# GQA attention into a gated MLP on one core: an earlier first half of v, later loads, statistics put behind the next weighing, and the last store issued by ScalarE

## The chip, the cores and the metric

The kernel runs on one core of one Trainium2 chip. The metric is the device time of one execution in microseconds. A core has five engines, each with its own in-order queue of instructions: TensorE (PE in the profile, with its weight loads as PEld), VectorE (DVE), ScalarE (ACT), GpSimd (POOL) and SyncE (SP), which here only issues DMAs. They wait for each other by semaphores.

## The reference

Eight batches of grouped-query attention (16 query heads on 4 key/value heads, 384 tokens, head size 64) give x of 384 x 1024 a batch. A gated MLP follows. What matters of it:

```python
attn = softmax(q @ k^T / 8)            # per head; k, v repeated for 4 query heads each
x = (attn @ v) as [B, S, 1024]
h = np.maximum(x @ w_in, 0.0)          # w_in: 1024 x 1024
u, v = h[..., :512], h[..., 512:]
mu = np.mean(v, axis=-1, keepdims=True)
var = np.mean((v - mu) ** 2, axis=-1, keepdims=True)
v_n = (v - mu) / np.sqrt(var + 1e-06)
v_s = np.einsum('ts,bsd->btd', w_spatial, v_n) + b_spatial[None, :, None]
return (u * v_s) @ w_out               # w_out: 512 x 1024
```

## The kernel before

The order of every engine's instructions is written out by hand. A main loop runs over 150 steps n. A batch b takes NU = 18 of them, from s0 = 18 b on: 6 groups m (three blocks of 128 query positions times two halves j of the heads) times 3 tiles t of keys. What a step issues, in this order:

- what `at(n, ...)` has put down for the step: DMA loads on SP's or GpSimd's queue, casts to 16 bit on GpSimd, and the DMA transposes `k_turn`, `q_turn` and `x_turn` on SP's queue;
- `scores`: two matmuls `sc` (L233, 64 rows each, side by side in the array) and one exponential of 128 x 1024 on ScalarE (L240). In batch 0 step n issues scores n + 1; later every even step issues its own and the next one's. There are two PSUM buffers `sc`;
- `weigh(b, m, hh)`, at n = s0 + 3 + 3 m + hh: twelve matmuls `av` of 65 columns (L247), then on VectorE the reciprocal `r` (L257) and the product `x` (L259). `av` has a single PSUM buffer, so the next `av` waits for `x`;
- what `turn_at(n, ...)` has put down: in the first batches transposes of k, q and x on TensorE (`kps`, `qps`, `xps`), copied out of PSUM by VectorE, and `keep_warm(4)`, four matmuls of 128 columns on the identity that nothing reads (L547);
- `run_fill(cols)`: takes matmuls of the MLP from one stream (`stream()`) until `cols` columns are paid.

The stream's order for batch 0 is v_tile(0,0), v_tile(0,1), u_tile(0,0), v_tile(0,2), u_tile(0,1), u_tile(0,2); then, per batch, the gates (`psp`), the first v_tile of the next batch, the output projection (`po`), and for later batches v_tile(b,1), v_tile(b,2) and the u blocks (`pu`). A `v_tile` is eight `pv` matmuls of 512 columns (L294), and on VectorE `vr` (L304), `stats` (L306) and the aggregate `mv` (L307). `normal(b)`, called out of the first u block (or the second u tile in batch 0), has ScalarE make `rstd` from the variance in two instructions (L314, L315), VectorE make `nmr` from it (L316), and GpSimd normalise the three tiles to `vn` (L327); in the last batch VectorE and ScalarE take one tile each.

All short-lived matmul results (`kps`, `qps`, `xps`, `wps`, `pv`, `pu`, `psp`, `po`) share one PSUM pool of three buffers, `ps_ck`. The tile `warm` is taken from it once at the start and stays held until the last `keep_warm`, at step 15.

The transposed x of batch b comes, from batch 1 on, by DMA transposes on SP's queue at steps s0 + 8, s0 + 14, s0 + 17 and s0 + 20 (one for each of the first two query blocks, two halves for the third). v_tile(b, st) reads block st. SP's queue also carries q's and k's transposes of the next batch, the loads of the batch after that (k, two halves of q, v) and the output stores.

How the fill is shared out in the first batch, with HV = 4096 columns for one v tile:

```python
run_fill(HV / 4 if 10 <= n < 14 else 2 * HV / 5 if 16 <= n else 0)   # n < NU + 3
```

Of the kernel before, what the change touches and what calls it, by code (L numbers as in the profile page):

```python
# [9 lines left out]
FP32 = mybir.dt.float32  # L10
FP16 = mybir.dt.float16
AF = mybir.ActivationFunctionType
ALU = mybir.AluOpType
# [4 lines left out]
def kernel(  # L18
# [16 lines left out]
    nc = tc.nc  # L35
    P = 128
    B, HQ, S, D = q.shape
# [4 lines left out]
    NT = S // P  # L42
# [181 lines left out]
    def scores(n):  # L224
        b, r = divmod(n, NU)
        m, t = divmod(r, NT)
        qt, j = divmod(m, 2)
        if t == 0:
            aTs[b, m] = att.tile([P, NT, 2, 512], FP16, name=f"aT_{b}_{m}", tag="aT", bufs=3)
        sc = ps_sc.tile([P, 2, 512], FP32, name=f"sc_{b}_{m}_{t}", tag="sc")  # L230
        for hh in range(2):
            half = slice(hh * D, (hh + 1) * D)
            nc.tensor.matmul(  # L233
                sc[:, hh],
                kTs[b][half, j, t * P : (t + 1) * P],
                qTs[b, j][half, qt],
                start=True,
                stop=True,
            )
        nc.scalar.activation(aTs[b, m][:, t], sc, AF.Exp, scale=scale)  # L240

    def weigh(b, m, hh):
        qt, j = divmod(m, 2)
        av = ps_av.tile([P, G, D + 1], FP32, name=f"av_{b}_{m}_{hh}", tag="av")
        for i in range(G):
            for t in range(NT):
                nc.tensor.matmul(  # L247
                    av[:, i, :],
                    aTs[b, m][:, t, hh, i * P : (i + 1) * P],
                    v1[b % 2][:, 2 * j + hh, t, 0 : D + 1],  # L250
                    start=(t == 0),
                    stop=(t == NT - 1),
                )
        if m == 0 and hh == 0:
            x16s[b] = att.tile([P, NT, NB, P], FP16, name=f"x16_{b}", tag="x16")
        r = small.tile([P, G, 1], FP32, name=f"r_{b}_{m}_{hh}", tag="r")
        nc.vector.reciprocal(r, av[:, :, D : D + 1])  # L257
        blk = 4 * j + 2 * hh
        nc.vector.tensor_tensor(  # L259
            x16s[b][:, qt, blk : blk + 2].rearrange("p k (i d) -> p (k i) d", i=2),  # L260
            av[:, :, 0:D],
            r.to_broadcast([P, G, D]),
            ALU.mult,
        )
# [23 lines left out]
    def v_tile(b, st):  # L288
        if st == 0:
            mvs[b] = small.tile([P, NT, 2], FP32, name=f"mv_{b}", tag="mv")  # L290
            v_rs[b] = []
        pv = ps_ck.tile([P, 512], FP32, name=f"pv_{b}_{st}", tag="ck")
        for kt in range(NB):
            nc.tensor.matmul(  # L294
                pv,
                x_tile(b)[:, st, kt],
                w_in16[:, kt, DH:DFF],
                start=(kt == 0),
                stop=(kt == NB - 1),
            )  # L300
            if kt < NB - 1:
                yield 512
        vr = moe.tile([P, DH], FP32, name=f"vr_{b}_{st}", tag="vr", bufs=4)
        nc.vector.tensor_scalar(vr, pv, 0.0, None, op0=ALU.max)  # L304
        stats = small.tile([P, 6], FP32, name=f"stats_{b}_{st}", tag="stats")
        nc.vector.bn_stats(stats, vr)  # L306
        nc.vector.bn_aggr(mvs[b][:, st, :], stats)  # L307
        v_rs[b].append(vr)
        yield 512

    def normal(b):
        rstd = small.tile([P, NT], FP32, name=f"rstd_{b}", tag="rstd")
        nmr = small.tile([P, NT], FP32, name=f"nmr_{b}", tag="nmr")
        nc.scalar.activation(rstd, mvs[b][:, :, 1], AF.Ln, bias=eps_t)  # L314
        nc.scalar.activation(rstd, rstd, AF.Exp, scale=-0.5)  # L315
        nc.vector.scalar_tensor_tensor(  # L316
            nmr, mvs[b][:, :, 0], -1.0, rstd, op0=ALU.mult, op1=ALU.mult
        )
        v_ns[b] = []
        for st in range(NT):  # L320
            vn = moe.tile([P, DH], FP16, name=f"vn_{b}_{st}", tag="vn", bufs=6)
            a, c = rstd[:, st : st + 1], nmr[:, st : st + 1]
            if b == B - 1 and st == 2:
                nc.scalar.activation(vn, v_rs[b][st], AF.Identity, scale=a, bias=c)
            else:
                by = nc.vector if b == B - 1 and st == 1 else nc.gpsimd
                by.tensor_scalar(vn, v_rs[b][st], a, c, op0=ALU.mult, op1=ALU.add)  # L327
            v_ns[b].append(vn)

    def uT_tile(b):  # L330
# [107 lines left out]
    def project(b, tt, half):  # L438
        last = b == B - 1
        rows = out[b].rearrange("(p t) d -> p t d", t=NT)  # L440
        if half == 0:
            osbs[b, tt] = ops.tile([P, DM], FP32, name=f"osb_{b}_{tt}", tag="osb")
        osb = osbs[b, tt]

        cuts = (512, 896, 1024) if last and tt == NT - 1 and half else (512 * half, 512 * half + 512)
        for i, (lo, hi) in enumerate(zip(cuts, cuts[1:])):
            po = ps_ck.tile([P, 512], FP32, name=f"po_{b}_{tt}_{half}_{i}", tag="ck")
            for m in range(NM):
                nc.tensor.matmul(  # L449
                    po[:, 0 : hi - lo],  # L450
                    gTs[b][:, m, tt * P : (tt + 1) * P],
                    w_out16[:, m, lo:hi],
                    start=(m == 0),
                    stop=(m == NM - 1),
                )
                if m < NM - 1:
                    yield hi - lo
            (nc.scalar.copy if half and not i else nc.vector.tensor_copy)(  # L458
                osb[:, lo:hi], po[:, 0 : hi - lo]
            )  # L460
            if last:
                nc.sync.dma_start(rows[:, tt, lo:hi], osb[:, lo:hi])
            elif half:
                nc.sync.dma_start(rows[:, tt, :], osb)
            yield hi - lo
# [66 lines left out]
    def at(n, f, *args):  # L532
        todo.setdefault(n, []).append((f, args))
# [6 lines left out]

    by_dve, by_act = nc.vector.tensor_copy, nc.scalar.copy

    warm = ps_ck.tile([P, 512], FP32, name="warm", tag="ck")

    def keep_warm(n):
        for _ in range(n):
            nc.tensor.matmul(warm[:, 0:P], ident16, ident16, start=True, stop=True)  # L547

# [27 lines left out]
    for j in range(2):  # L576
        for t in (1, 2):
            turn_at(3 * (2 * t + j) - 3, q_transposes, 0, j, t, by_dve)
    for n in (*range(10), 14, 15):
        turn_at(n, keep_warm, 4)  # L580
    at(9, cast_k, 1, pool)
    at(10, cast_q, 1, 0, pool)
# [19 lines left out]
    for b in range(B):  # L602
        s0 = NU * b
        if b >= 2:
            w0 = s0 - NU
            if b > 2:
                at(w0 - NU + 11, load_k, b)
                at(w0 - NU + 11, load_q, b, 0)
                at(w0 - NU + 11, load_q, b, 1)
                at(w0 - NU + 11, load_v, b)  # L610
            c0, c1, t0, t1 = (6, 7, 10, 12) if b > 2 else (9, 10, 12, 13)
            at(w0 + c0, cast_k, b, pool)
            at(w0 + c0, cast_q, b, 0, pool)
            at(w0 + c1, cast_q, b, 1, pool)
            at(w0 + c1, cast_v, b, pool)
            at(w0 + t0, k_turn, b)
            at(w0 + t0, q_turn, b, 0)
            at(w0 + t1, q_turn, b, 1)
        for m in range(6):
            if b == 0 or b == B - 1 and m > 3:  # L620
                turn_at(s0 + 3 * m + 5 + (m < 5 and b == 0), x_transposes, b, m)
            elif m in (1, 3):
                at(s0 + 3 * m + 5, x_turn, b, m // 2, 0, NB)
            elif m > 3:
                at(s0 + 3 * m + 5, x_turn, b, 2, 4 * (m - 4), 4 * (m - 3))
# [5 lines left out]
    def run_fill(cols):  # L631
        nonlocal owed
        owed += cols
        while owed > 0:
            owed -= next(fill, 1e9)

    for n in range(total + 6):
        for f, args in todo.pop(n, []):
            f(*args)
        if n + 1 < NU:  # L640
            scores(n + 1)
        elif n >= NU and n % 2 == 0 and n < total:
            scores(n)
            scores(n + 1)
        for hh in range(2):
            b, r = divmod(n - 3 - hh, NU)
            if n >= 3 + hh and r % 3 == 0 and b < B:
                weigh(b, r // 3, hh)
        for f, args in turns.pop(n, []):
            f(*args)  # L650
        if n < NU + 3:

            run_fill(HV / 4 if 10 <= n < 14 else 2 * HV / 5 if 16 <= n else 0)
        elif n < 2 * NU + 4:
            run_fill((4 * HV + NM * NT * S + 6 * NM * 512) / (NU + 4 - 3))
        else:
            run_fill(COLS / NU)
# [31 lines left out]
```

## Time and profile before

| | us |
|---|---|
| median of 3 runs (lowest, highest) | 251.71 (251.39, 252.03) |
| the profiled execution, its own time | 251.51 |
| its span, first to last instruction | 249.7 |

| engine | busy us | share of the span |
|---|---|---|
| TensorE matmuls | 240.9 | 96% |
| ScalarE | 169.1 | 68% |
| VectorE | 139.9 | 56% |
| GpSimd | 97.4 | 39% |

Times in all views are microseconds from the span's start; a duration that follows an operation as a mean is in nanoseconds. In the time line a row is start, length, engine, line, operation, output <- input, shapes, count, and in brackets the idle time before it with what ended it. In the chain of waits a row is start, length, engine and line. In the list of waits a row is who waited for whom: total, times, longest. In the table of windows a row is the stretch, its length, then the busy time of TensorE, its weight loads, VectorE, ScalarE and GpSimd with the numbers of instructions, the granted clock, the share of the DMA engines and GB/s. A matmul's record is longer than its turn: matmuls are pipelined, and two neighbours overlap.

### The profile page before, as it was taken

To read this page: it belongs to the slowest core of one execution; us is meant where nothing else is said; L and a number is where in the kernel's file an instruction comes from. 1 tells how busy PE (TensorE), PEld (TensorE's weight loads), DVE (VectorE), ACT (ScalarE), POOL (GpSimd) and SP (SyncE) were. 2 spreads that over 40 slices of the span, in tenths; PEclk is the share of its full clock that TensorE was granted. 3 is DMA by queue.
4 is the path that set the end of the run, shared out by engine and by line. 5 is a ranking of instruction groups with operands and counts; after the bars stand their busy time and mean duration, and the time that the engine had idled before them with its cause. 6 is when DMAs were issued, how large, how long until landed. Compare 5 with 4: busy or idle time off the path is not lost.

```text
span 249.7 us, 6038 instructions
## 1 busy us (share of the span) xinstructions
PE 240.9 (96%) x2438; PEld 126.2 (51%) x2438; DVE 139.9 (56%) x370; ACT 169.1 (68%) x217; POOL 97.4 (39%) x141
## 2 busy tenths in 40 slices
PE   7998998999999999999999999999999999999993
PEld 7564666634455445544455445544455444554551
DVE  2455777764546646375536746375536746375662
ACT  3896665777686677868686677868686687862231
POOL 2698836881034800393034800393034000350130
PEclk9999999999999999999999999999999999999999
DMA  7999998999379973996479973999474172024206
GB/s 180 269 285 252 301 281 238 289 233 265 104 145 326 173 276 66 236 274 178 168 145 333 169 273 71 206 302 175 171 151 90 24 273 45 0 46 168 84 26 230
DMA packets 73980, 46.93 MB, mean 188 GB/s; under 512 B 48112, under 2 KB 68912, under 8 KB 73952
## 3 DMA queue, kind: packets, MB, share of 16 engines
q1 hardware_dynamic: 68832, 37.63, 59.2%
q0 software_dynamic: 4080, 8.65, 13.9%
q8 instruction: 19, 0.31, 0.5%
q10 hardware_dynamic: 1040, 0.26, 0.5%
q14 instruction: 9, 0.07, 0.1%
HBM read 25.95 MB, written 12.58 MB: 154 GB/s over the span
## 4 chain that ended last, share of the span: by engine, by line
PE 91%; DVE 6%; ACT 1%; issue 1%; POOL 0%; POOLq 0%
PE av L247 17%; PE pv L294 16%; PE sc L233 15%; PE po L449 15%; PE pu L359 14%; PE psp L378 6%; PE warm L547 3%; DVE x L259 2%; DVE stats L306 1%; DVE vr L304 1%; PE pu L342 1%; PE qps L200 1%; ACT aT L240 1%; PE psp L402 1%; PE xps L275 1%
## 5 line engine op out<-in xcount | busy, mean ns | idle before, releaser
L240 ACT ACTIVATE aT<-sc 128x1024 f16<-128x1024 f32 x144 | 139.6, 1021 | 53.3 <-PE sc L233 53.1
L247 PEld LDWEIGHTS <-aT 128*128 128x128 f16 x1152 | 43.4, 97 | 32.9 <-DVE x L259 12.8
L327 POOL TENSOR_SCALAR vn<-vr,rstd,nmr 128x512 f16<-128x512 f32 x22 | 16.9, 778 | 100.0 <-DVE r L257 86.2
L247 PE MATMUL av<-v,aT 128*128 128x65 f16 x1152 | 52.4, 194 | 1.6 <-DVE x L259 1.2
L257 DVE RECIPROCAL r<-av 128x4 f32<-128x4 f32 x96 | 17.2, 179 | 58.3 <-PE av L247 57.7
L294 PE MATMUL pv<-w_in,xt 128*128 128x512 f16 x192 | 49.6, 379 | 0.0
L449 PE MATMUL po<-w_out,gT 128*128 128x512 f16 (+2 forms) x196 | 47.9, 375 | 0.0
L233 PE MATMUL sc<-qT,kT 64*128 64x512 f16 x288 | 45.4, 385 | 0.5 <-DVE qT L205 0.3
L259 DVE TENSOR_TENSOR x<-av,r 128x256 f16<-128x256 f32 x96 | 40.8, 425 | 3.4
L359 PE MATMUL pu<-xt,w_in 128*128 128x384 f16 x216 | 40.2, 326 | 0.0
L389 POOL TENSOR_TENSOR gT<-g,uT 128x384 f16<-128x384 f32 x28 | 24.7, 914 | 26.8 <-DVE g L388 26.8
L359 PEld LDWEIGHTS <-w_in 128*128 128x128 f16 x216 | 19.4, 98 | 14.2 <-issue 2.5
L170 POOL CAST q<-q 128x768 f16<-128x768 f32 (+1 forms) x36 | 24.9, 733 | 3.1 <-DMA q<-in_q_dram 3.1
L449 PEld LDWEIGHTS <-gT 128*128 128x128 f16 x196 | 16.9, 97 | 18.3 <-issue 2.9
L294 PEld LDWEIGHTS <-xt 128*128 128x128 f16 x192 | 16.1, 97 | 13.5 <-issue 0.6
L458 DVE COPY osb<-po 128x512 f32<-128x512 f32 (+1 forms) x25 | 16.7, 667 | 11.1 <-PE po L449 11.1
L233 PEld LDWEIGHTS <-kT 64*128 64x128 f16 x288 | 8.9, 94 | 26.4 <-issue 24.0
L304 DVE TENSOR_SCALAR vr<-pv 128x512 f32<-128x512 f32 x24 | 16.5, 688 | 10.2 <-PE pv L294 10.0
L458 ACT COPY osb<-po 128x512 f32<-128x512 f32 (+1 forms) x24 | 14.0, 584 | 10.6 <-PE po L449 10.5
L306 DVE BATCH_NORM_STATS2 stats<-vr 128x6 f32<-128x512 f32 x24 | 16.7, 695 | 0.8
L378 PE MATMUL psp<-wsT,vn 128*128 128x384 f16 x84 | 17.0, 327 | 0.0
L388 DVE TENSOR_TENSOR g<-psp,bias_b 128x384 f32<-128x384 f32 x28 | 14.4, 552 | 2.7 <-PE psp L378 2.7
(59 smaller groups left out, 136.2 us busy)
## 6 DMA issues: line engine op xcount, KB each, us to landing
out_dram<-osb SPq DMA_DIRECT2D x21, 512.0 KB, 2.9
q<-in_q_dram SPq DMA_DIRECT2D x10, 768.0 KB, 7.1
q<-in_q_dram POOLq DMA_DIRECT2D x4, 768.0 KB, 10.4
v<-in_v_dram SPq DMA_DIRECT2D x6, 384.0 KB, 8.7
w_in<-in_moe_w_in_dram POOLq DMA_DIRECT2D x4, 512.0 KB, 9.8
k<-in_k_dram SPq DMA_DIRECT2D x5, 384.0 KB, 4.1
out_dram<-osb SPq DMA_DIRECT2D x5, 256.0 KB, 2.0
q<-in_q_dram SPq DMA_DIRECT2D x2, 512.0 KB, 7.2
```

The costliest lines, as they stand in the source:

```text
L170: f(q16s[b, j][:, lo:hi, :, hh, :], src[:, hh, lo:hi])
L233: nc.tensor.matmul(sc[:, hh], kTs[b][half, j, t * P : (t + 1) * P], qTs[b, j][half, qt], start=True, stop=True,)
L240: nc.scalar.activation(aTs[b, m][:, t], sc, AF.Exp, scale=scale)
L247: nc.tensor.matmul(av[:, i, :], aTs[b, m][:, t, hh, i * P : (i + 1) * P], v1[b % 2][:, 2 * j + hh, t, 0 : D + 1], start=(t == 0), stop=(t ...
L259: nc.vector.tensor_tensor(x16s[b][:, qt, blk : blk + 2].rearrange("p k (i d) -> p (k i) d", i=2), av[:, :, 0:D], r.to_broadcast([P, G, D]) ...
L294: nc.tensor.matmul(pv, x_tile(b)[:, st, kt], w_in16[:, kt, DH:DFF], start=(kt == 0), stop=(kt == NB - 1),)
L306: nc.vector.bn_stats(stats, vr)
L359: nc.tensor.matmul(pu[:, 0:S].rearrange("p (t s) -> p t s", t=NT), w_in16[:, kt, m * P : (m + 1) * P], x_tile(b)[:, :, kt], start=(kt == 0 ...
L378: nc.tensor.matmul(psp[:, 0:S], v_ns[b][st][:, m * P : (m + 1) * P], wsT16[:, st, :], start=(st == 0), stop=(st == NT - 1),)
L389: nc.gpsimd.tensor_tensor(gTs[b][:, m, :], g, uTs[b][:, m, :], ALU.mult)
L449: nc.tensor.matmul(po[:, 0 : hi - lo], gTs[b][:, m, tt * P : (tt + 1) * P], w_out16[:, m, lo:hi], start=(m == 0), stop=(m == NM - 1),)
L458: (nc.scalar.copy if half and not i else nc.vector.tensor_copy)(osb[:, lo:hi], po[:, 0 : hi - lo])
```

## The change

Five things, in one diff:

- A v tile's `stats` and aggregate aren't issued at once but put into a list `due`, which is emptied after the next `weigh`, before the next v tile's `vr`, or at the head of `normal`. In the last batch they are issued at once.
- `normal` makes `minus` = -mean, which doesn't need `rstd`, in place of `nmr`; the normalisation adds `minus` and multiplies by `rstd`. The last batch makes one [128 x 1] product `ac` more, for ScalarE's tile.
- The first v tile's eight `pv` are spread over steps 6 to 11, the second's over 13 to 17, the third share over 18 to 20. Scores 13 to 17 are issued one step later, 14 with 15 and 16 with 17. `keep_warm` runs at steps 0 to 5 alone and takes a PSUM buffer anew each time.
- The loads of batches 3 to 7 are issued at step 16 of a period of 18, in place of step 11: on SP's queue behind the second half of q's transposes and the second x transpose, ahead of the last two x transposes.
- The very last store (128 columns, 64 KB) is issued by ScalarE in place of SyncE.

```diff
@@ v_tile
+        do_due()
         vr = moe.tile([P, DH], FP32, name=f"vr_{b}_{st}", tag="vr", bufs=4)
         nc.vector.tensor_scalar(vr, pv, 0.0, None, op0=ALU.max)
         stats = small.tile([P, 6], FP32, name=f"stats_{b}_{st}", tag="stats")
-        nc.vector.bn_stats(stats, vr)
-        nc.vector.bn_aggr(mvs[b][:, st, :], stats)
+
+        def statistics():
+            nc.vector.bn_stats(stats, vr)
+            nc.vector.bn_aggr(mvs[b][:, st, :], stats)
+
+        due.append(statistics)
+        if b == B - 1:
+            do_due()
         v_rs[b].append(vr)
         yield 512
 
+    due = []
+
+    def do_due():
+        while due:
+            due.pop(0)()
+
@@ normal
         rstd = small.tile([P, NT], FP32, name=f"rstd_{b}", tag="rstd")
-        nmr = small.tile([P, NT], FP32, name=f"nmr_{b}", tag="nmr")
+        do_due()
+        minus = small.tile([P, NT], FP32, name=f"minus_{b}", tag="minus")
         nc.scalar.activation(rstd, mvs[b][:, :, 1], AF.Ln, bias=eps_t)
         nc.scalar.activation(rstd, rstd, AF.Exp, scale=-0.5)
-        nc.vector.scalar_tensor_tensor(
-            nmr, mvs[b][:, :, 0], -1.0, rstd, op0=ALU.mult, op1=ALU.mult
-        )
+        nc.vector.tensor_scalar(minus, mvs[b][:, :, 0], -1.0, None, op0=ALU.mult)
+        if b == B - 1:
+            ac = small.tile([P, 1], FP32, name="ac", tag="ac")
+            nc.vector.tensor_tensor(ac, minus[:, 2:3], rstd[:, 2:3], ALU.mult)
...
-            a, c = rstd[:, st : st + 1], nmr[:, st : st + 1]
+            a, c = minus[:, st : st + 1], rstd[:, st : st + 1]
             if b == B - 1 and st == 2:
-                nc.scalar.activation(vn, v_rs[b][st], AF.Identity, scale=a, bias=c)
+                nc.scalar.activation(vn, v_rs[b][st], AF.Identity, scale=c, bias=ac)
             else:
                 by = nc.vector if b == B - 1 and st == 1 else nc.gpsimd
-                by.tensor_scalar(vn, v_rs[b][st], a, c, op0=ALU.mult, op1=ALU.add)
+                by.tensor_scalar(vn, v_rs[b][st], a, c, op0=ALU.add, op1=ALU.mult)
@@ project
             if last:
-                nc.sync.dma_start(rows[:, tt, lo:hi], osb[:, lo:hi])
+                (nc.scalar if i else nc.sync).dma_start(rows[:, tt, lo:hi], osb[:, lo:hi])
@@ the schedule
-    warm = ps_ck.tile([P, 512], FP32, name="warm", tag="ck")
-
     def keep_warm(n):
+        warm = ps_ck.tile([P, 512], FP32, name="warm", tag="ck")
         for _ in range(n):
             nc.tensor.matmul(warm[:, 0:P], ident16, ident16, start=True, stop=True)
...
-    for n in (*range(10), 14, 15):
+    for n in range(6):
         turn_at(n, keep_warm, 4)
...
-                at(w0 - NU + 11, load_k, b)
-                at(w0 - NU + 11, load_q, b, 0)
-                at(w0 - NU + 11, load_q, b, 1)
-                at(w0 - NU + 11, load_v, b)
+                at(w0 - NU + 16, load_k, b)
+                at(w0 - NU + 16, load_q, b, 0)
+                at(w0 - NU + 16, load_q, b, 1)
+                at(w0 - NU + 16, load_v, b)
@@ the main loop
-        if n + 1 < NU:
+        if n < 12:
             scores(n + 1)
-        elif n >= NU and n % 2 == 0 and n < total:
+        elif n == 13:
+            scores(n)
+        elif n % 2 == 0 and n > 13 and n < total:
             scores(n)
             scores(n + 1)
...
                 weigh(b, r // 3, hh)
+                do_due()
...
-            run_fill(HV / 4 if 10 <= n < 14 else 2 * HV / 5 if 16 <= n else 0)
+            at_n = {6: 8, 7: 8, 8: 8, 9: 8, 10: 4, 11: 4, 13: 6, 14: 6, 15: 6, 16: 4, 17: 4}
+            run_fill(HV / at_n[n] if n in at_n else HV / 3 if n >= NU else 0)
```

## The prediction

> **What bounds the kernel now.** I read the page first (busy time, clock), then the waits, then a table of windows, then the time line around every place where TensorE stands still.
>
> ```profile
> span 249.7 us, 6038 instructions
> ...
> PE 240.9 (96%) x2438; PEld 126.2 (51%) x2438; DVE 139.9 (56%) x370; ACT 169.1 (68%) x217; POOL 97.4 (39%) x141
> ...
> PEclk9999999999999999999999999999999999999999
> ...
> L240 ACT ACTIVATE aT<-sc 128x1024 f16<-128x1024 f32 x144 | 139.6, 1021 | 53.3 <-PE sc L233 53.1
> ...
> 95.28:123.34 28.06, 28.02 (x273) 13.65 (x273) 15.58 (x41) 20.83 (x28) 10.60 (x14) 1.00 0.82 205
> ...
> PE av L247 <- DVE x L259: 1.2, 3, 0.6
> ```
>
> TensorE is busy for 240.9 of 249.7 us; the next engine, ScalarE, for 169.1. The window is one batch in the steady part: 28.06 us, 28.02 of them busy on TensorE. So nothing is won by making another engine faster; only by taking work off TensorE or by ending one of its few waits. The wait named, 1.2 us in three places, is for x on VectorE. "Busy" hides more: a matmul's record outlasts its turn in the pipe, so a short stall leaves no gap. It shows when starts are compared with the pace.
>
> ```profile
> 229.86 3.45 PE pv L294 x16
> 28.74 0.54 PE sc L233 x4
> ...
> 119.12 2.10 PE L294 MATMUL pv<-w_in,xt 128*128 128x512 f16 x9
> 122.08 1.24 PE L294 MATMUL pv<-w_in,xt 128*128 128x512 f16 x5
> 123.34 0.55 PE L247 MATMUL av<-v,aT 128*128 128x65 f16 x12
> 99.66 0.60 PE L233 MATMUL sc<-qT,kT 64*128 64x512 f16 x4
> 100.28 0.54 PE L247 MATMUL av<-v,aT 128*128 128x65 f16 x12
> ...
> 99.51 0.16 DVE L316 SCALAR_TENSOR_TENSOR nmr<-mv,rstd 128x3 f32<-128x3 f32 x1 [1.45 <-ACT rstd L315]
> 99.80 0.42 DVE L259 TENSOR_TENSOR x<-av,r 128x256 f16<-128x256 f32 x1
> 121.12 0.69 DVE L304 TENSOR_SCALAR vr<-pv 128x512 f32<-128x512 f32 x1 [1.16 <-PE pv L294]
> 121.84 0.69 DVE L306 BATCH_NORM_STATS2 stats<-vr 128x6 f32<-128x512 f32 x1
> 122.67 0.15 DVE L257 RECIPROCAL r<-av 128x4 f32<-128x4 f32 x1
> 122.86 0.42 DVE L259 TENSOR_TENSOR x<-av,r 128x256 f16<-128x256 f32 x1
> ```
>
> Sixteen pv take 3.45 us, 0.216 each. Five from 122.08 are through at 123.16, but the av behind them starts at 123.34: it waits for x, which ends at 123.28, because the PSUM buffer of av is single and VectorE did vr and the statistics first. That is a stall of 0.18. Likewise four sc take 0.54, so av could start at 100.20 and starts at 100.28: x (99.80 + 0.42 = 100.22) was held up since nmr stood waiting for rstd at the head of VectorE's queue. 0.08. Together 0.26 us a batch, invisible on the page.
>
> **The change, part by part.** *Statistics behind the next weighing.* In the new program's order r and x stand ahead of stats and aggregate except in the last batch, and what takes the place of nmr needs no rstd, so VectorE doesn't stand behind ScalarE. In the first stall above, r starts when vr ends (121.81) or its av does, and x ends before 123.0, ahead of 123.16; what is late next is nothing, as stats then fills the room before the next av ends. In the second, the wait of 1.45 us is gone and x is done long before 100.20. The trace has it six times (the av of 123.34 less two and plus three periods of 28.06, from 67.2 to 207.5): 6 x 0.26 = 1.56 us off. Bounds: 1.1 (first kind alone, 6 x 0.18) to 1.6. Batch 1 has two larger ones:
>
> ```profile
> 40.23 0.55 PE L247 MATMUL av<-v,aT 128*128 128x65 f16 x12 [0.58 <-DVE x L259]
> 54.37 0.54 PE L247 MATMUL av<-v,aT 128*128 128x65 f16 x12 [0.43 <-DVE x L259]
> ```
>
> The second is a plain case of statistics ahead of x: 0.43 off. Before the first, vr, stats, aggregate and the wait for rstd stand in a row; the flush at the head of the normalisation keeps the statistics ahead of x there, and only the wait goes. I take 0.55 of it (0.4 to 0.7, with the unseen part of the stall). The third of the 1.2 us, in the last batch, stays, as the statistics aren't put off there. Batch 1: 0.98 off. The new [128x1] product in the last batch costs what nmr did (0.16) and stands in its place: 0.
>
> *The early half of v.* Eight of the first pv move from steps 10 to 13 into steps 6 to 11, the filler matmuls of steps 6 to 9, 14 and 15 go, scores 13 to 17 come a step later with 14/15 and 16/17 in pairs, and the filler's PSUM buffer is no longer held through to step 15.
>
> ```profile
> 13.39 0.48 PE av L247 x12
> 14.09 0.22 PE warm L547 x4
> 14.32 0.22 PE xps L275 x4
> 15.89 0.33 PE warm L547 x4
> 26.21 0.32 PE sc L233 x2
> ...
> 14.80 0.41 DVE L276 COPY xt<-xps 128x512 f16<-128x512 f16 x1
> ...
> 21.65 0.38 PE L275 MATMUL xps<-ident,x 128*128 128x128 f16 x4 [0.84 <-DVE qT L205]
> ```
>
> Off: four fillers of 0.22 and two of 0.33 that all lay on TensorE's path, 1.5 us; a pair costs 0.54 against twice 0.32, 0.2 for two; the wait of 0.84 for a free buffer. Some 2.6 us. On: waits for VectorE, which I follow step by step. Step 6 without its filler is through with xps at 14.31. The first pv needs the copy xt, which still ends at 14.80 + 0.41 = 15.21: it starts at 15.27, a stall of 0.95, and sc 8 stands behind it. Steps 7 to 11 are five sc (1.60), three av (1.44), a qps and an xps (four transposes each, 0.44) and seven pv (1.51): through at 20.48, with all eight pv done where before had four. Step 12 (av, qps, xps, 0.92) ends at 21.40. On VectorE vr runs from 20.65 (a record ends 0.16 after its turn) to 21.34, then r and x (122.67 to 123.28 above, 0.61) to 21.95: after sc 13 the next av waits 0.3 and ends at 22.5. Behind x come stats and aggregate (121.84 to 122.67, 0.83) and the copies of qT and xt (0.41 each), to 23.5 with their overlap, and the pv of step 13, the first of the second tile, needs that xt: another 1.0. Two pv, the pair 14/15 (with a kps), one pv: 24.9. Step 15's av needs the exponentials of score 14, ready at about 24.3 + 1.02 (a wait of 0.45); av behind it ends at 25.8; two kps, a qps and an xps (0.8) share two free buffers and so wait for VectorE's copies (0.6 to 0.8 more); two pv follow, and step 16 starts near 27.8. Pair, av, qps and four pv later, step 18 starts at 29.9, against 28.74. So the waits put on, 3.4 to 3.8, eat more than the 2.6 taken off: 1.2 later. By then 16 pv are done against 14.4 (8 and two shares of 3.2), worth 1.6 x 0.216 = 0.35, which the smaller shares of steps 18 to 20 give back. I take 0.9 us on. Bounds: 0.3 (the two long xt waits a third shorter) to 1.4 (nothing given back).
>
> The fillers were there to keep TensorE running. The first 27 took 3.06 us, 0.113 each, those later 0.22 / 4 = 0.055: it starts at half rate, though PEclk reads 9.
>
> ```profile
> 1.62 3.06 PE warm L547 x27
> ```
>
> The gap of 0.84 was followed by xps and pv at full rate. The longest new one is 0.95 with pv and av on both sides, so I put no loss of rate into the sum. The Trainium skill, "TensorE: Matmul & The Clock Gate", Part 1, says that the gate halves the clock after an idle window of some 3.4 us; by that rule too single gaps of 1 us cost nothing, though what it counts is activity over a window. The stretch from 21.7 to 27.8 has three waits, so half rate is a rival below.
>
> *Loads five steps later.* Four loads a batch (five batches) now stand on SP's queue behind qT and the second x transposition, ahead of the last two.
>
> ```profile
> 68.52 1.24 SPq L279 DMA_TRANSPOSE xt<-x  x1
> 72.74 0.88 SPq L79 DMA_DIRECT2D k<-in_k_dram  x1
> 74.92 1.98 SPq L82 DMA_DIRECT2D v<-in_v_dram  x1
> 76.99 5.65 SPq L215 DMA_TRANSPOSE qT<-q  x1
> 87.24 1.34 SPq L279 DMA_TRANSPOSE xt<-x  x1
> ...
> v<-in_v_dram SPq DMA_DIRECT2D x6, 384.0 KB, 8.7
> xt<-x SPq DMA_TRANSPOSE x26, 3.2
> ```
>
> A step is 28.06 / 18 = 1.56 us. The second x transposition, six steps behind the one at 68.52, can now go at 77.9, and the loads at 79.2 instead of 72.74: v is issued at 81.4 and lands at 90.1. The third is issued behind it and, held like qT was (5.65), is through the queue by 89; 3.2 later it has landed, 92.2 at the latest. The ninth pv of 119.12 needs it, at 120.85, here 92.79. The fourth follows a store at about 89.5 and lands at 92.7 to 93.5; it is needed three pv after 122.08, here 94.67. Hidden, with 0.6 and 1.2 us to spare: 0. The cover is thin; in batch 1, where two stores stand between, it may lack 0 to 0.7 once (I take 0.1).
>
> *Last store on ScalarE's queue.*
>
> ```profile
> 245.72 1.30 SPq L462 DMA_DIRECT2D out_dram<-osb  x3
> 245.87 0.29 DVE L458 COPY osb<-po 128x128 f32<-128x128 f32 x1 [0.18 <-PE po L449]
> ...
> out_dram<-osb SPq DMA_DIRECT2D x1, 192.0 KB, 2.2
> out_dram<-osb SPq DMA_DIRECT2D x1, 64.0 KB, 1.9
> ```
>
> The copy ends at 246.16; SP issues the 64 KB store 0.40 before 247.02, so at 246.62, landing at 248.5. On its own queue it could go at 246.2. But the 192 KB store, issued about 0.45 ahead of it and landing 2.2 later, at 248.3, then ends the run: 0.15 off (0 to 0.4).
>
> Sum: 0.9 + 0.1 - 0.98 - 1.56 - 0.15 = -1.7. The profiled execution took 251.51, its span of 249.7 and 1.8 around it, which I leave: 249.8. The median of the runs, 251.71, stands 0.2 above it, so a median would come at 250.0; I take 249.9.
>
> **Rivals.** *Late transpositions (slower).* For: qT behind the loads took 5.65 to issue, and the fourth x transposition now also has a store ahead of it. If both drain at that pace, it starts at 90 to 94 and lands as much as 3 us too late for its pv, in each of five batches. At 1 us each: +5.0 - 1.7, so 254.9; at 0.35 the gain is gone. Against: each has a third of qT's blocks, and 3.2 to landing is the median of 26 that share the queue with loads and stores. *Stalls only move (no change).* Statistics behind x now push the next g, osb and vr, whose three PSUM buffers TensorE also needs, and the early part costs its 1.4: 251.5. For: four waits in the early part are of this kind. Against: in 28 us VectorE has 12 free. *Half rate.* If TensorE falls back once, for as long as the first 27 fillers ran so (3.06), it does 1.5 us less: 251.4. By the rule of the Trainium skill, "TensorE: Matmul & The Clock Gate", Part 1, it would come so only if a whole window there counted as idle.
>
> **How the numbers follow.** Forecast 0.70, faster; stalls only move 0.12 and half rate 0.03, no change; late transpositions 0.15, slower. A measurement here can tell about 0.3%, 0.75 us, from no change. The forecast's costs at all their best ends give 0.3 - 1.13 - 1.6 - 0.4 = -2.8, at all their worst 1.4 + 0.7 - 0.83 - 1.1 = +0.2, which is the no-change case. The range, 249.0 to 251.8, takes in that case, and leaves out the late transpositions and the last few tenths at the best end.
>
> **What would show it.** Right: the two pv-to-av and sc-to-av stalls gone from each batch, which shrinks from 28.06 to 27.8; av's wait for x down from three to one or two; new waits of about 1 us for xt near 14.3 and 22.5, and step 18's scores at about 29.9. Wrong: TensorE waiting for a transposition (a pv with a gap before it once a batch), or 128-column matmuls at 0.11 us behind step 12.

## The result, and the profile after

The changed kernel takes 250.09 us in the median of 7 runs (249.34 to 250.23), the kernel before in the same comparison 251.47 (7 runs, 251.26 to 252.03). The ratio is 0.9935, with a 95% interval of 0.9921 to 0.9948: 1.4 us less, where 1.7 had been forecast. The profiled execution took 250.14, its span is 248.4 (before 251.51 and 249.7).

First the page of the changed kernel: span, and busy time by engine; then the table of windows for the batch that answers to the one shown of before.

```profile
span 248.4 us, 5987 instructions
...
PE 238.2 (96%) x2414; PEld 125.3 (50%) x2414; DVE 140.4 (57%) x371; ACT 168.9 (68%) x217; POOL 98.2 (40%) x141
...
95.01:122.78 27.77, 27.77 (x274) 13.72 (x273) 15.68 (x42) 20.81 (x28) 10.74 (x14) 1.00 0.85 206
```

TensorE lost 2.7 us of busy time, but the span only 1.3. The 2.7 are the fillers and also the short stalls, which count as busy (28.02 in the batch shown before, 27.77 here). The time in which TensorE stands idle grew from 8.8 to 10.2. The share of 96% tells nothing of that. A steady batch takes 27.77 in place of 28.06, and TensorE is busy in all of it. The time line shows how; the first four rows are TensorE, the rest VectorE:

```profile
99.37 0.60 PE L233 MATMUL sc<-qT,kT 64*128 64x512 f16 x4
99.90 0.54 PE L247 MATMUL av<-v,aT 128*128 128x65 f16 x12
...
121.70 1.24 PE L294 MATMUL pv<-w_in,xt 128*128 128x512 f16 x5
122.78 0.54 PE L247 MATMUL av<-v,aT 128*128 128x65 f16 x12
...
98.71 0.42 DVE L259 TENSOR_TENSOR x<-av,r 128x256 f16<-128x256 f32 x1
120.74 0.69 DVE L305 TENSOR_SCALAR vr<-pv 128x512 f32<-128x512 f32 x1 [1.16 <-PE pv L294]
121.90 0.18 DVE L257 RECIPROCAL r<-av 128x4 f32<-128x4 f32 x1 [0.47 <-PE av L247]
122.12 0.42 DVE L259 TENSOR_TENSOR x<-av,r 128x256 f16<-128x256 f32 x1
122.46 0.68 DVE L309 BATCH_NORM_STATS2 stats<-vr 128x6 f32<-128x512 f32 x1
```

Five pv now start 1.08 ahead of the av behind them, which is five times 0.216; before it was 1.26. Four sc start 0.53 ahead of theirs, before 0.62. x ends at 99.13 and 122.54, before av needs it, and the statistics run behind it. The 0.47 that VectorE stands waiting at r costs TensorE nothing.

The early part is where the waits are. The list of waits of TensorE, and the time line around the places that it names:

```profile
PE pv L294 <- DVE xt L276: 1.9, 2, 1.0
...
PE av L247 <- DVE x L259: 0.4, 2, 0.2
...
PE pv L294 <- DMA xt<-x: 0.2, 1, 0.2
```

```profile
13.89 0.39 PE L275 MATMUL xps<-ident,x 128*128 128x128 f16 x4
15.23 0.39 PE L294 MATMUL pv<-w_in,xt 128*128 128x512 f16 x1 [0.95 <-DVE xt L276]
22.28 0.55 PE L247 MATMUL av<-v,aT 128*128 128x65 f16 x12 [0.19 <-DVE x L259]
23.74 0.60 PE L294 MATMUL pv<-w_in,xt 128*128 128x512 f16 x2 [0.90 <-DVE xt L276]
25.78 0.49 PE L247 MATMUL av<-v,aT 128*128 128x65 f16 x10 [0.35 <-ACT aT L240]
27.27 0.38 PE L275 MATMUL xps<-ident,x 128*128 128x128 f16 x4 [0.60 <-DVE kT L193]
27.49 0.38 PE L294 MATMUL pv<-w_in,xt 128*128 128x512 f16 x1
29.90 0.72 PE L233 MATMUL sc<-qT,kT 64*128 64x512 f16 x4
66.79 0.60 PE L294 MATMUL pv<-w_in,xt 128*128 128x512 f16 x2 [0.17 <-DMA xt<-x]
```

av waits for x only 0.4 us in place of 1.2, and two waits of 0.9 to 1.0 for the copy xt have come in. The last row is one that the prediction had put at 0.1: a pv that waits for a DMA transpose, in batch 1 alone.

To see where time goes, the start of one and the same matmul is compared in two kernels, which also shows stalls that leave no gap in the records. For this and all experiments, in us against the kernel before (minus is earlier), with the place in the kernel before on top:

| kernel | first scores 6.43 | av 13.33 | step 18's scores 28.67 | scores 35.02 | av 40.23 | av 54.37 | batch 2's first scores 56.35 | av 67.23 | av 207.51 |
|---|---|---|---|---|---|---|---|---|---|
| the change | +0.01 | -0.04 | +1.22 | +0.92 | +0.35 | -0.16 | -0.15 | 0.00 | -1.41 |
| e1 statistics put off, alone | -0.18 | -0.38 | -0.01 | -0.33 | -0.33 | -0.83 | -0.42 | -0.60 | -1.58 |
| e2 `minus`, alone | +0.01 | +0.01 | +0.01 | +0.01 | -0.55 | -0.56 | -0.24 | -0.24 | -0.65 |
| e3 early half, alone | -0.58 | +0.08 | +1.48 | +1.57 | +1.57 | +1.58 | +2.26 | +2.26 | +2.27 |
| e4 loads at step 16, alone | -0.18 | -0.40 | -0.40 | -0.39 | -0.39 | -0.39 | -0.39 | -0.39 | -0.41 |
| e5 the change, no early half | -0.34 | -0.31 | +0.06 | -0.25 | -0.81 | -1.32 | -1.32 | -0.45 | -1.86 |
| e6 statistics and `minus` | +0.01 | 0.00 | +0.37 | +0.05 | -0.52 | -1.02 | +0.27 | +0.09 | -1.32 |
| e7 the change, v one step later | +0.01 | +0.01 | -1.45 | -1.29 | -1.86 | -2.36 | -2.36 | -1.03 | -2.44 |
| e8 no early half, fillers away, loads at 13 | -0.39 | -0.23 | -1.67 | -1.99 | -2.56 | -3.06 | -3.06 | -3.14 | -4.55 |
| e9 the change, loads at 13 | +0.10 | +0.10 | +1.38 | +1.08 | +0.51 | +0.02 | +0.02 | -0.17 | -1.58 |
| e10 last store on ScalarE, alone | +0.01 | -0.11 | -0.11 | -0.11 | -0.11 | -0.11 | -0.10 | -0.11 | -0.09 |
| e11 buffer, loads at 13 | 0.00 | 0.00 | -0.99 | -0.99 | -0.99 | -0.99 | -0.99 | -0.99 | -0.98 |

Up to 13.89 TensorE's order of matmuls is the same in all these kernels, so what stands in the first two columns is not of the edits (the last section says where it comes from). What happens ahead of step 18 is therefore read from av 13.33 on: the change loses 1.26 there. Steps within a row are read, not its end.

### The profile page after: what moved, and what is told of

Read it like the earlier page. It is cut to its first block, busy times and chain, and to the rows that moved or that the text cites. A ratio compares the mean times of both kernels' runs of the same rounds, so it can differ in the third digit from the quotient of the medians.

```text
span 248.4 us, 5987 instructions
## 1 busy us (share of the span) xinstructions
PE 238.2 (96%) x2414; PEld 125.3 (50%) x2414; DVE 140.4 (57%) x371; ACT 168.9 (68%) x217; POOL 98.2 (40%) x141
## 4 chain that ended last, share of the span: by engine, by line
PE 89%; DVE 4%; DMA 2%; ACT 1%; issue 1%; POOL 0%; POOLq 0%
PE av L247 16%; PE pv L294 16%; PE po L466 15%; PE sc L233 15%; PE pu L376 14%; PE psp L395 6%; DMA xt<-x 2%; PE warm L563 2%; PE pu L359 2%; ACT aT L240 1%; DVE x L259 1%; PE qps L200 1%; PE psp L419 1%; DVE qT L205 1%; DVE vr L305 1%; PE xps L275 1%
## 5 line engine op out<-in xcount | busy, mean ns | idle before, releaser
L247 PEld LDWEIGHTS <-aT 128*128 128x128 f16 x1152 | 44.1, 97 | 30.3 <-issue 13.4
L344 POOL TENSOR_SCALAR vn<-vr,minus,rstd 128x512 f16<-128x512 f32 x22 | 17.0, 784 | 79.3 <-ACT rstd L331 79.3
L233 PE MATMUL sc<-qT,kT 64*128 64x512 f16 x288 | 44.9, 383 | 0.7 <-ACT aT L240 0.4
L405 DVE TENSOR_TENSOR g<-psp,bias_b 128x384 f32<-128x384 f32 x28 | 14.4, 551 | 2.7 <-PE psp L395 2.7
```

What stands on the lines that cost most here:

```text
L233: nc.tensor.matmul(sc[:, hh], kTs[b][half, j, t * P : (t + 1) * P], qTs[b, j][half, qt], start=True, stop=True,)
L247: nc.tensor.matmul(av[:, i, :], aTs[b, m][:, t, hh, i * P : (i + 1) * P], v1[b % 2][:, 2 * j + hh, t, 0 : D + 1], start=(t == 0), stop=(t ...
```

## The experiments

The theory was the prediction's: the statistics and `minus` bring 0.26 us a batch and about 1 in batch 1; the early half of v costs 0.9; the loads cost next to nothing; the store brings a little. The rivals were that the early half is itself a gain, that the loads at step 16 cost time in every batch, and that stalls only move. e1 to e4 share one set of runs of the kernel before, e5 to e8 a second, e9 to e11 a third.

**e1: the statistics put off, and nothing else.**

```diff
+        do_due()
         vr = moe.tile([P, DH], FP32, name=f"vr_{b}_{st}", tag="vr", bufs=4)
...
-        nc.vector.bn_stats(stats, vr)
-        nc.vector.bn_aggr(mvs[b][:, st, :], stats)
...
+        due.append(statistics)
...
                 weigh(b, r // 3, hh)
+                do_due()
```

> The kernel before with the statistics behind the next weighing alone. Theory (the stalls on VectorE's order): the 0.18 us stall of av behind pv goes in six batches and the 0.43 us one in batch 1, 1.1 + 0.43 = 1.5 us off, so about 250.0; the period falls from 28.06 to 27.88, and the stall of 0.08 behind sc stays. Rival (the later loads, or the early half, bring the gain): 251.5, the stall moves to another av, g or osb.

Measured: 250.40 against 251.57, ratio 0.9957 (0.9934 to 0.9981), 0.4 short of what was expected. From av 67.23 to av 207.51 it gains 0.98 in five batches, 0.196 each: the stall behind pv, predicted at 0.18. In batch 1 the wait before av 54.37 goes (-0.33 to -0.83), but 0.41 of it is lost at the next scores, by the time line:

```profile
55.93 0.61 PE L233 MATMUL sc<-qT,kT 64*128 64x512 f16 x4 [0.34 <-ACT osb L472]
```

The row puts it down to ScalarE's osb. e2 and e6, with a loss at the same scores, name the transposed q, which comes by DMA, and the landings agree with them: the first half of q lands at 55.79 in e1, 55.97 in e2 and 56.48 in e6, each time 0.14 ahead of these scores.

**e2: `minus` in place of `nmr`, and nothing else.**

```diff
-        nc.vector.scalar_tensor_tensor(
-            nmr, mvs[b][:, :, 0], -1.0, rstd, op0=ALU.mult, op1=ALU.mult
-        )
+        nc.vector.tensor_scalar(minus, mvs[b][:, :, 0], -1.0, None, op0=ALU.mult)
...
-                by.tensor_scalar(vn, v_rs[b][st], a, c, op0=ALU.mult, op1=ALU.add)
+                by.tensor_scalar(vn, v_rs[b][st], a, c, op0=ALU.add, op1=ALU.mult)
```

> The kernel before with minus in place of nmr alone. Theory: VectorE no longer stands behind rstd: 0.08 us in each of six batches and about 0.55 in batch 1, so 1.0 off, about 250.5; the stalls of 0.18 behind pv stay. Rival (VectorE's queue only waits one place later): 251.5.

Measured: 251.03, ratio 0.9978 (0.9967 to 0.9989). 0.55 at av 40.23, just the term of the sum, and 0.08 a batch from 67.23 on (0.41 in five). It stays half a microsecond short of the time expected; 0.32 of that is lost at batch 2's first scores, where -0.56 becomes -0.24. The time line of e2:

```profile
53.81 0.54 PE L247 MATMUL av<-v,aT 128*128 128x65 f16 x12 [0.43 <-DVE x L259]
56.11 0.61 PE L233 MATMUL sc<-qT,kT 64*128 64x512 f16 x4 [0.25 <-DMA qT<-q]
```

The wait for x of 0.43 at the first row is the statistics' part and is still there. The second row is new.

**e3: the early half of v, and nothing else** (with the fillers, their buffer and the order of scores that belong to it).

```diff
-    for n in (*range(10), 14, 15):
+    for n in range(6):
         turn_at(n, keep_warm, 4)
...
-            run_fill(HV / 4 if 10 <= n < 14 else 2 * HV / 5 if 16 <= n else 0)
+            at_n = {6: 8, 7: 8, 8: 8, 9: 8, 10: 4, 11: 4, 13: 6, 14: 6, 15: 6, 16: 4, 17: 4}
+            run_fill(HV / at_n[n] if n in at_n else HV / 3 if n >= NU else 0)
```

> The kernel before with the early half of v alone (fill, fillers, paired scores, filler's PSUM buffer). Theory: two waits of about 1 us for xt near 14.3 and 22.8 and three smaller ones outweigh the fillers taken off: 0.9 to 1.4 us slower, about 252.6, step 18's scores at 29.9 against 28.7. Rival (fewer fillers and paired scores are the gain): 0.9 us faster, 250.6.

Measured: 253.63, ratio 1.0076 (1.0059 to 1.0093), 2.1 us slower, 1.0 more than expected. The rival that it is a gain falls. It costs more alone than in the change; its list of waits and its time line:

```profile
PE av L247 <- DVE x L259: 2.6, 5, 1.1
...
PE sc L233 <- DMA qT<-q: 0.6, 1, 0.6
```

```profile
23.33 0.55 PE L247 MATMUL av<-v,aT 128*128 128x65 f16 x12 [1.11 <-DVE x L259]
58.61 0.61 PE L233 MATMUL sc<-qT,kT 64*128 64x512 f16 x4 [0.61 <-DMA qT<-q]
```

The statistics of the first tile, not put off, stand ahead of x, and av waits 1.11 at 23.33, where the change shows 0.19. That makes little difference by itself: the change waits 0.90 for xt at the next pv, e3 no second time, and up to step 18 e3 loses 1.40 where the change loses 1.26. The larger part comes at batch 2's first scores, which the transposed q holds up (+1.58 to +2.26, a wait of 0.61), although these come later than in any other kernel.

**e4: the loads at step 16, and nothing else.**

```diff
-                at(w0 - NU + 11, load_k, b)
...
+                at(w0 - NU + 16, load_k, b)
```

> The kernel before with the loads five steps later alone. Theory: hidden; no change within 0.3 us but for a wait of some 0.3 us for xt in batch 1, so 251.5 to 251.9. Rival (transposes free of the loads make the steady batches shorter): 1.5 us faster, 250.0, with a period below 28.06.

Measured: 251.35, ratio 1.0000 (0.9984 to 1.0015). No change in time, as expected; its row in the table is flat from 13.33 on, so the wait of 0.3 us for xt in batch 1, expected too, is not there. The rival of late transposes in every batch falls with it.

**e5: the change without the early half.** The schedule's part of the diff is undone (fillers, their buffer, order of scores, fill; the last is shown); the statistics, `minus`, the loads at 16 and the store stay.

```diff
...
-            at_n = {6: 8, 7: 8, 8: 8, 9: 8, 10: 4, 11: 4, 13: 6, 14: 6, 15: 6, 16: 4, 17: 4}
-            run_fill(HV / at_n[n] if n in at_n else HV / 3 if n >= NU else 0)
+            run_fill(HV / 4 if 10 <= n < 14 else 2 * HV / 5 if 16 <= n else 0)
```

> The changed kernel with the early half of v undone (fill, fillers, scores and the filler's buffer as before), all else kept. Theory: the early half costs about 0.9 us in the change, so this is 1.0 to 1.3 us faster than it, near 248.9. Rival (fewer fillers are part of the gain): slower than the change, near 251.

Measured: 250.31 against 251.45, ratio 0.9946 (0.9924 to 0.9968). This is a miss: 248.9 was expected, and without the part that costs 0.9 the kernel is no faster than with it (0.9935). The table has the reason: it leads by 1.32 at batch 2's first scores and by 0.45 at av 67.23. Its time line there:

```profile
66.33 0.60 PE L294 MATMUL pv<-w_in,xt 128*128 128x512 f16 x2 [0.88 <-DMA xt<-x]
```

The DMA transpose of x arrives late, and the larger part of the lead won ahead of it is spent waiting.

**e6: statistics and `minus` together, loads at step 11 as before, store by SyncE.** Beside e5, only the loads' place and the store differ.

> The same as the one without the early half, but with the loads at step 11 and the last store on SP, as before. Theory (the first scores of batch 2 wait for q's transpose, which stands behind the loads at step 11, so that what is won ahead of 55 us is given back there): a wait of nearly 1 us at the first scores of batch 2, some 0.6 us slower than the one without the early half, near 249.5. Rival (the loads' place is worth nothing, as when moved alone): the same as that one, near 248.9.

Measured: 249.81, ratio 0.9925 (0.9901 to 0.9950), 0.3 from the 249.5 expected. But it was to be slower than e5, and the two intervals overlap, so no difference is shown. Its lead is spent elsewhere, by its time line on TensorE and then on SyncE's queue:

```profile
56.62 0.61 PE L233 MATMUL sc<-qT,kT 64*128 64x512 f16 x4 [1.22 <-DMA qT<-q]
```

```profile
44.84 2.25 SPq L82 DMA_DIRECT2D v<-in_v_dram  x1
47.20 2.76 SPq L208 DMA_TRANSPOSE kT<-k  x1
50.06 5.78 SPq L215 DMA_TRANSPOSE qT<-q  x2
```

With the loads at step 11 the transposes of k and q for batch 2 stand behind them, and the queue is through with the last of them at 55.84. The half of q that batch 2's first scores need lands at 56.48, and they wait 1.22. With the loads at step 16 (e5) there is no such wait, but the one for x.

**e7: the change with v's shares one step later.** If the early half costs time since each pv asks for xt in the step in which it is copied, one step should do.

```diff
-            at_n = {6: 8, 7: 8, 8: 8, 9: 8, 10: 4, 11: 4, 13: 6, 14: 6, 15: 6, 16: 4, 17: 4}
-            run_fill(HV / at_n[n] if n in at_n else HV / 3 if n >= NU else 0)
+            at_n = {7: .125, 8: .125, 9: .125, 10: .125, 11: .25, 12: .25, 14: 1/6, 15: 1/6, 16: 1/6, 17: .25, 18: .5, 19: 3/8, 20: 3/8}
+            run_fill(HV * at_n.get(n, 0))
```

> The changed kernel with every share of v's fill one step later (steps 7 to 12, 14 to 17, the rest over 18 to 20), nothing else changed. Theory (what costs is that pv is asked for in the step in which its xt is still being copied): the waits of 0.95 and 0.9 us for xt go, step 18's scores come near 27.9 in place of 29.9, and the total is 1.5 to 2.2 us below the change, near 248.2. Rival (TensorE has the same work, the waits come back elsewhere before step 21): within 0.4 us of the change.

Measured: 248.21, ratio 0.9865 (0.9835 to 0.9894). Both waits for the copy xt are gone, and step 18's scores start 2.67 earlier than in the change (-1.45 against +1.22), at 27.22, where 27.9 was expected. Of a lead of 2.36 at 56.35 then only 1.03 is left at 67.23, which was not expected. So the cause is borne out, but that the time is just the one expected is in part luck. Its list of waits:

```profile
PE pv L294 <- DMA xt<-x: 1.2, 2, 0.9
```

**e8: no early half, but its other parts, and the loads at step 13.** The kernel before with statistics, `minus`, the store by ScalarE, and:

```diff
-    warm = ps_ck.tile([P, 512], FP32, name="warm", tag="ck")
     def keep_warm(n):
+        warm = ps_ck.tile([P, 512], FP32, name="warm", tag="ck")
...
-    for n in (*range(10), 14, 15):
+    for n in range(6):
...
-                at(w0 - NU + 11, load_k, b)
+                at(w0 - NU + 13, load_k, b)
```

> A version put together from the parts: the fill and the scores as before, fillers at steps 0 to 5 alone with a PSUM buffer taken anew each time, statistics put off, minus, the last store on ScalarE, and the loads two steps after q's first transposes (step 13), ahead of the second x transpose. Theory: the wait for a buffer at 20.8 (1.0 us with its start) and 1.3 us of fillers go, the stalls on VectorE's order go, and neither q's nor x's transposes stand behind the loads at a bad time: 4 us below the kernel before, near 247.3. Rival (TensorE then waits for loads or ScalarE's exponentials in batch 0): near 249.

Measured: 247.36, ratio 0.9838 (0.9808 to 0.9867): 4.1 us faster than the kernel before and, as its interval lies below that of the change, faster than the change. The time line of SyncE's queue:

```profile
40.75 1.94 SPq L208 DMA_TRANSPOSE kT<-k  x1
42.80 4.05 SPq L215 DMA_TRANSPOSE qT<-q  x2
46.94 0.82 SPq L79 DMA_DIRECT2D k<-in_k_dram  x1
...
49.05 3.19 SPq L82 DMA_DIRECT2D v<-in_v_dram  x1
52.33 4.78 SPq L279 DMA_TRANSPOSE xt<-x  x2
```

The transposes of k and q go ahead of the loads and those of x behind them, and neither holds TensorE: its list of waits has no DMA for scores or pv, and the lead of 3.06 at 56.35 is 3.14 at 67.23. The interval overlaps that of e7, so the times don't tell these two apart.

**e9: the change with the loads at step 13.** The same one number, in the change itself.

> The changed kernel with the loads at step 13 (behind q's transposes, ahead of the second x transpose) in place of step 16, nothing else changed. Theory (in batch 1 the loads at step 16 hold up the last x transposes): the wait of pv for xt at 66.8 (0.34 us) goes and nothing else moves, about 0.3 us below the change, near 249.8. Rival (at step 13 the second x transpose comes late instead): a new wait at the pv of the tile before, the same time or more.

Measured: 249.63 against 251.67, ratio 0.9918 (0.9890 to 0.9945). The interval overlaps that of the change, so the time alone doesn't tell the two apart. The trace shows the wait gone: pv has no gap before the av at 67.06, by its time line, and 0.19 is won between 56.35 and 67.23, where the change loses 0.15.

```profile
65.98 1.24 PE L294 MATMUL pv<-w_in,xt 128*128 128x512 f16 x5
67.06 0.54 PE L247 MATMUL av<-v,aT 128*128 128x65 f16 x12
```

**e10: the last store issued by ScalarE, and nothing else.**

```diff
-                nc.sync.dma_start(rows[:, tt, lo:hi], osb[:, lo:hi])
+                (nc.scalar if i else nc.sync).dma_start(rows[:, tt, lo:hi], osb[:, lo:hi])
```

> The kernel before with the last store issued by ScalarE alone. Theory: the 192 KB store beside it then ends the run, 0 to 0.2 us off, not to be told from no change: 251.3 to 251.5. Rival (the issue time on SP is what ends the run): 0.4 us off, 251.1, with the last landing 0.4 us nearer to the last copy.

Measured: 251.64 against 251.67, ratio 0.9996 (0.9979 to 1.0014). No gain. The time line of e10, then its list of DMA issues:

```profile
245.78 0.29 DVE L458 COPY osb<-po 128x128 f32<-128x128 f32 x1 [0.18 <-PE po L449]
246.10 0.36 ACTq L462 DMA_DIRECT2D out_dram<-osb  x1
```

```profile
out_dram<-osb SPq DMA_DIRECT2D x1, 192.0 KB, 2.3
...
out_dram<-osb ACTq DMA_DIRECT2D x1, 64.0 KB, 2.4
```

The store goes out at 246.10 and not at 246.62 (0.09 of that is the copy, which is earlier in this profile), but takes 2.4 to land and not 1.9: 248.5 both times. It lands 0.16 to 0.19 behind the 192 KB store in all thirteen profiles, whether it is issued 0.46 to 0.47 behind it by SyncE or 0.04 by ScalarE.

**e11: the filler's PSUM buffer taken anew, all fillers kept, loads at step 13.** What the buffer is worth by itself.

> The kernel before with the fillers' PSUM buffer taken anew each time (all fillers kept) and the loads at step 13. Theory: with three buffers for the transposes and pv, TensorE's wait at 20.8 (1.0 us with its start) goes: about 1.0 us off, near 250.5, step 18's scores at 27.6. Rival (VectorE's copy is late whatever the buffers): 251.4, the wait stays.

Measured: 250.51, ratio 0.9956 (0.9936 to 0.9977). The lead of 0.99 comes in one go at the place of the wait for a free buffer (0.84 in the kernel before), well ahead of the first load that was moved, and no later wait eats it: the time line shows xps with no wait ahead of it.

```profile
20.65 0.39 PE L275 MATMUL xps<-ident,x 128*128 128x128 f16 x4
```

## Why the prediction came out nearly right

**Stalls in the steady batches: right.** 0.28 a batch in the change, 1.41 in the five batches between av 67.23 and av 207.51. e1 and e2 divide it as predicted: 0.20 behind pv (predicted 0.18), 0.08 behind sc (0.08). Nothing came late in their place, so the rival that stalls only move falls for the steady batches.

**Batch 1: right in size.** Predicted 0.98. In the change 0.57 goes at av 40.23 and 0.51 at av 54.37, together 1.08. e2 alone shows the first (0.55), e1 alone the second (0.50).

**Early half: right in size, with one part counted wrong.** The predicted waits of 0.95, 0.3, 1.0, 0.45 and 0.6 to 0.8 are in the time line as 0.95, 0.19, 0.90, 0.35 and 0.60, and step 18 starts at 29.90, where 29.9 was said. Then 0.35 was to be given back by the smaller shares of steps 18 to 20, and 0.30 is (1.22 to 0.92). But the shares account for less: ahead of step 18's scores 16 pv are done in the change and 15, not 14.4, in the kernel before, and 20 in both ahead of scores 35.02. That is one pv, 0.22. The same stretch also holds a stall that goes with the statistics: e1, whose shares are those of before, gains 0.32 in it. Its time line, with the place where it had lost as much just before:

```profile
26.73 0.38 PE L200 MATMUL qps<-ident,q 128*128 128x128 f16 x4 [0.16 <-DVE kT L193]
...
32.45 0.40 PE L275 MATMUL xps<-ident,x 128*128 128x128 f16 x4
```

and the second place in the kernel before:

```profile
32.47 0.71 PE L275 MATMUL xps<-ident,x 128*128 128x128 f16 x4
```

In e1 the statistics, now behind x, stand ahead of the copy of kT, for which qps waits: from av 26.47 to step 18's scores e1, e5 and e6 lose 0.42 each. Behind step 18 the four xps take 0.31 less. So in batch 0 the stall mostly moves, as the rival said it would everywhere.

**Loads: mis-sized, and the step was wrong in kind.** The term was 0.1 once, "hidden" otherwise. In the steady batches hidden is right. The time line of SyncE's queue in the change shows the last two transposes of x:

```profile
83.50 2.50 SPq L279 DMA_TRANSPOSE xt<-x  x1
...
87.14 1.50 SPq L279 DMA_TRANSPOSE xt<-x  x1
```

The third is through the queue at 86.0, where 89 had been allowed, and the fourth goes in at 87.14, where 89.5 had been. Neither takes the 3.2 to landing that the prediction used: it is 6.5 and 4.5 from their issue. The two errors work against each other, and the transposes land at 89.97 and 91.64, ahead of the 92.2 and 92.7 to 93.5 predicted. In batch 1 the change loses 0.16 between av 54.37 and av 67.23, where e9, without the wait, wins 0.19: 0.35. Its chain of waits (start, length, what) and the queue show the row that does it:

```profile
60.85 5.89 DMA xt<-x
```

```profile
51.22 2.08 SPq L279 DMA_TRANSPOSE xt<-x  x1
...
55.20 2.05 SPq L82 DMA_DIRECT2D v<-in_v_dram  x1
57.34 2.32 SPq L279 DMA_TRANSPOSE xt<-x  x1
59.76 1.00 SPq L481 DMA_DIRECT2D out_dram<-osb  x2
60.85 2.11 SPq L279 DMA_TRANSPOSE xt<-x  x1
```

The last transpose of x is issued at 60.85, behind the loads, another transpose and two stores, and lands at 66.74; the pv goes at 66.79. The prediction took for each term a price of its own and added. In batch 1 that doesn't hold: the DMA sets a time for batch 2's first scores (loads at 11) or for the last pv of v (loads at 16), and a gain won ahead of it counts hardly beyond that time. With the loads at 11 the first half of q lands between 55.79 and 56.48 in the kernel before, e1, e2 and e6, though they stand up to 1.02 apart at av 54.37. With the loads at 16 the last transpose of x lands at 66.74 in the change, 66.29 in e5 and 65.70 in e7, which are 1.16 and 2.20 further ahead at av 54.37. So e5, which saves the 0.9 of the early half, waits 0.88 instead, and e7 loses 1.33 of its lead. The one number is free of charge by itself (e4) and decides how much of a lead passes batch 1: 0.45 of 1.32 in e5 and 1.03 of 2.36 in e7 with the loads at 16, nothing of 1.02 in e6 with the loads at 11, all of 3.06 in e8 with the loads at 13. The step that failed is "it may lack 0 to 0.7 once (I take 0.1)": 0.35 lies within the bounds, but it was no price of the loads; it grows with what is won ahead of it, to 0.88 in e5.

**Store: wrong.** 0.15 was said, nothing came (e10). The step that failed is that the 192 KB store would end the run: the 64 KB store still lands 0.16 behind it in e10, at 248.5. In the change the last copy starts 1.52 earlier than before (244.35 against 245.87), the store goes out at 244.68, 1.94 earlier, and with 2.4 to land in place of 1.9 ends about 1.4 earlier. The Trainium skill, "DMA: Bandwidth & Descriptors", "Issuing engines are not separate DMA queues", says that DMAs share the same 16 engines whoever issues them, so that a second issuer saves only issue time. The trace agrees as far as it goes: the earlier issue in e10 bought nothing. That the engines are shared is not shown by a run here.

**The sum.** Early half +0.92, batch 1 -1.08, the late transpose +0.16 (0.35 less the stall of that batch), steady batches -1.41, the last scores' stall in batch 7 some -0.10, the store's lost time +0.1: -1.4, and the profiled executions differ by 1.37. The forecast's -1.7 is 0.3 off: the store and the loads came out 0.25 worse each, batch 1 and the stalls of the later batches some 0.1 better each.

**The rivals.** Late transposes in every batch: not seen, in e4 or the change. Half rate: not seen; behind the waits of 0.95, 0.90 and 0.60 four transposes of 128 columns from 27.27 on are through when the pv starts at 27.49: 0.22 for four, as in the kernel before at 14.32. By the rule that the prediction cited from the Trainium skill, "TensorE: Matmul & The Clock Gate", Part 1, single waits of 1 us should not halve the clock; the trace agrees.

What the prediction didn't see is that the early half costs by its steps, and not by being early. From av 13.33 to step 18's scores the change loses 1.26, and nearly the same shares one step later (e7) win 1.46. That is as much as the fill of before with some fillers away and the buffer free (e8, 1.44); the buffer alone is worth 0.99 of it (e11). In batch 1 e7 then loses 1.33 of its lead, with the loads at step 16, and e8 nothing, with the loads at 13. e7 with the loads at 13 was not run, so which of the two fills is the better one is not shown.

## What to carry to other kernels

Compare the start of the same matmul in two kernels: a stall of 0.2 us that leaves no gap in the records, and a gain that is lost again later, show only there. Terms of a sum add only where nothing downstream is fixed by another resource: before adding, find the next time that a DMA queue sets, and ask whether the gain reaches past it. A move that is neutral by itself (the loads here) may take or save a part of another gain, so try it together with that gain.

## What was not expected of the hardware

- A transpose behind loads on the same queue is slow to issue and holds what stands behind it. The two of q took 5.78 us in SyncE's queue behind the loads in e6 (4.86 to 5.93 in the six kernels with that order), and 4.05 ahead of them in e8 (3.29 to 4.05 in seven).
- The last store's landing time did not follow its issue: 0.52 us earlier out, landed at the same 248.5 (e10). It came 0.16 to 0.19 behind the 192 KB store ahead of it in all thirteen profiles. That it waits for that store is likely, but no run leaves that store out.
- With the same order of matmuls on TensorE, batch 0's first scores start anywhere from 5.85 (e3) to 6.53 us (e9). The traces show where it comes from: matmuls of 128 columns start 0.107 us apart at first and 0.056 apart later, and the step from one to the other comes at 4.5 us in e5, 4.6 in e3, 5.1 in e8, 5.9 in e1, 6.0 in e4, and behind 6.2 in the others. At av 13.33 the profiles still lie between -0.40 and +0.10, so one profile against another is good to 0.5 us, unless the comparison starts behind that place. Why the step comes when it does, no run here shows.
